# Who computes the second half's input operands, and in which steps

## The chip, the core and the metric

The kernel runs on one core of a Trainium2 chip. A core has a matrix engine (PE), a vector engine (DVE), a scalar engine (ACT), a GpSimd engine (POOL) and a queue engine (SP) that issues DMAs; they run side by side, each in the order of its own queue, and wait for each other by semaphores. The metric is the device time of one execution in microseconds (us), the median of several runs. The engines work on SBUF (128 partitions); PE writes to PSUM, a small memory with banks of 128x512 floats.

## The reference

A gate g mixes two branches over the same input x (2048 tokens, 576 features):

```
g = sigmoid((x * gate_w).sum(-1))
a = linear attention (32 heads, two softmaxes as feature map) @ wo
b = (relu(x @ W_gate) * (x @ W_up)) @ W_down        # 576 -> 4608 -> 576
out = g * a + (1 - g) * b
```

Everything is float32. Branch b is the larger part of the work and the only one that the change touches.

## The kernel before, in words

**Precision.** PE multiplies in a shortened form of float32 ("fp32r"). Each operand is therefore kept as a rounded high part, made by ACT, and a low part (operand minus high part), made by DVE; a product is high x high + high x low + low x high.

**Branch b.** The tokens fall into two halves of 1024, the features into two halves, and the products are done by a scheme of seven block products in place of eight (Strassen's). For this each half of the tokens needs seven operands, made from four blocks of x: the blocks are scaled with a row of square roots of 1 - g (in the tile that the profile calls `ac` here, `sb` in the code), three blocks are used as they are and four operands are differences. Each operand is then split into high and low parts. The operands of the second half are made while the first half is computed, by the generator `second_half` (line 1283 and on): it loads four blocks of 128x512 into `xr` tiles (b11, b12, b21, b22), scales them (line 1311), forms the four differences in place (line 1315), rounds (line 1316, ACT) and forms the low part (line 1296, or 1299 for a third of it), and stores the pair to DRAM (`xod`, 512 KB a time). Both parts pass through one tile `o`, so a new rounding must wait until the store before it has been read out. All of this happens three times, once for each p = 0, 1, 2 (three slices of 128 rows): 12 products with the root row, 12 differences, 21 roundings, 21 low parts, 21 stores.

**Units and steps.** A unit u is one block of 128 hidden features of one half of the tokens; units 0 to 35 are the first half, 36 to 71 the second. A unit has seven steps j = 0 to 6, one for each block product, in function `step`. In a step PE does seven matmuls of the block product (line 1145, into the banks `cx`, `ca`, `cy`) and three to five of the down projection of an earlier unit pair (line 1176, into `pd` and `pm`). DVE, ACT and POOL meanwhile turn finished banks into hidden values and split them (lines 1276, 1281, 1346, 1354, 1404, 1502), add up outputs (1242), and split the weights of coming units (ACT 876 and 1107, DVE 879, 882, 897 to 900, 1110, and POOL 1096 to 1099 for sums of down weights). An even unit has more hidden values to split than an odd one. From unit 36 on the weights are read back from DRAM and this extra work is gone.

**What sets the order.** The whole stage stands in `in_order`: every engine executes its instructions in the order in which the code was traced. An engine doesn't stop at the end of a step; it runs ahead until an instruction's semaphore holds it. At the end of `step` stands the call that advances `second_half`: before the change after steps 3 and 6 of each unit from 4 to 33, 60 calls at most. Between two `yield`s lies what one call issues. One p takes 18 calls, so nine units: the loads (first call), products of t = 0 two calls on, products of t = 1 and the first rounding two calls on, then low part and (difference and) rounding in turn. The last low part comes in unit 30.

Two places where PE can be held matter later: the product of step 6 adds to bank `cx`, which DVE's line 1404 in step 5 has to have read; and the down matmuls of a step need the low part from line 1281 of the step before and a bank that ACT (line 1225) has filled.

Of the kernel before, what the change touches and what calls it, by code (L numbers as in the profile page):

```python
# [1 line left out]

# [7 lines left out]
AF = mybir.ActivationFunctionType  # L10
# [6 lines left out]
TB = 512  # L17
NTB = S // TB
NT = S // P
NC = F // P  # L20
# [63 lines left out]
def gated_mix_kernel(  # L84
# [24 lines left out]
    nc = tc.nc  # L109
    PSUM = bass.MemoryType.PSUM  # L110
    SUB, ADD, MULT = ALU.subtract, ALU.add, ALU.mult
    tt, pt = nc.vector.tensor_tensor, nc.gpsimd.tensor_tensor
# [10 lines left out]
    sbd = dram.tile([P, NTB, TB], F32, name="sbd")  # L123
# [350 lines left out]
    with in_order(tc, nc, nc.gpsimd):  # L474
        for t in range(2, NT - 2):
            if t in (3, 6, 10):
                load_x((t + 2) // 4)
            if t == 8:
                whole(half_gates(0))
                sb = xw.tile([P, 2, TB], F32, name="sb", bufs=1)  # L480
# [180 lines left out]
    t = NT - 1  # L661
# [450 lines left out]
    def rest_weights(g, step):  # L1112

        a = WDR[g, 0][:, 4 * P:].rearrange("p (c q) -> p c q", c=2)
        if step == 0:
            nc.scalar.activation(W4[g][:, 0:2, 0], a, AF.Copy)
        elif step == 1:
            tt(out=W4[g][:, 0:2, 1], in0=a, in1=W4[g][:, 0:2, 0].bitcast(F32), op=SUB)  # L1118
            pt(out=a[:, 0], in0=a[:, 0], in1=a[:, 1], op=ADD)  # L1119
        elif step == 2:  # L1120
            nc.scalar.activation(W4[g][:, 2, 0], a[:, 0], AF.Copy)
            nc.scalar.activation(W4[g][:, 3], W4[g][:, 1].bitcast(F32), AF.Copy, scale=-1.0)
        else:
            tt(out=W4[g][:, 2, 1], in0=a[:, 0], in1=W4[g][:, 2, 0].bitcast(F32), op=SUB)
# [30 lines left out]
    def load_rest(hf):  # L1155
        for t in range(2):
            a = ACC4[hf, t] = sums_of[0][64 * t:64 * (t + 1), 2]
            nc.sync.dma_start(a, att[4 * P:, rows(0, 0, t, hf)[1]])
# [128 lines left out]
    def second_half():  # L1287

        sb = sums_of[2][:, 2]
        ra, rb_ = (xr.tile([P, 3, TB], F32, name="xr", tag="xr") for _ in range(2))  # L1290
        b11, b12, b21, b22 = b = ra[:, 0], ra[:, 1], ra[:, 2], rb_[:, 0]
        o = rb_[:, 1:3].bitcast(F32R)

        def low(n, p, a):
            if p < 2:
                tt(out=o[:, 1], in0=a, in1=o[:, 0].bitcast(F32), op=SUB)
                nc.sync.dma_start(xod[:, n - 1, p::3], o.bitcast(F32))
            else:
                tt(out=o[32:64, 0], in0=a[32:64], in1=o[32:64, 0].bitcast(F32), op=SUB)
                nc.sync.dma_start(xod[:, n - 1, p], o[:, 0].bitcast(F32))  # L1300

        for p in range(3):
            for i, a in enumerate(b):
                k, t = divmod(i, 2)
                nc.sync.dma_start(a, xs[:, k, p, (2 + t) * TB:(3 + t) * TB])
            for t in range(2):
                nc.sync.dma_start(sb, sbd[:, 2 + t])
                yield
                yield
                for a in b[t::2]:  # L1310
                    tt(out=a, in0=a, in1=sb, op=MULT)
            for n, r, a, c in ((1, b11, None, None), (2, b21, None, None), (3, b22, None, None), (5, b11, b12, b11),
                               (7, b12, b22, b12), (6, b22, b22, b11), (4, b21, b21, b22)):
                if a is not None:
                    tt(out=r, in0=a, in1=c, op=SUB)
                nc.scalar.activation(o[:, 0], r, AF.Copy)
                yield
                low(n, p, r)
                yield

    def swap_in(u, j):

# [28 lines left out]
    def gate_last(up, g, made):  # L1351

        if made:
            tt(out=g, in0=up, in1=g, op=MULT)
        else:
            gated(g, up)
        return g
# [31 lines left out]
    def step(u, j):  # L1389


        g, odd = divmod(u, 2)
# [16 lines left out]
        make = 0 < u < NC - 1  # L1409
        old = not odd and g > 0  # L1410

        if j == 0:
            if u > 0:
                a = gate_last(*LATE.pop())
# [85 lines left out]
        elif j == 6:  # L1500
            a = T["g2"]
# [48 lines left out]
        if u == NC + 1:  # L1550
            if j == 6:
                store_rest(0, 0)
                store_rest(0, 1)
                load_rest(1)
        if j in (3, 6) and 4 <= u < NC - 2:
            next(later_half, None)

    later_half = second_half()
    with in_order(tc, nc, nc.tensor, nc.vector, nc.scalar, nc.gpsimd, nc.sync):
        for u in range(len(units)):  # L1560
            for j in range(7):
                step(u, j)
# [152 lines left out]
```

## Time and profile before

| what | value |
|---|---|
| median of 3 runs | 1566.52 us (1566.35 to 1567.34) |
| the profiled execution, its own time | 1565.42 us |
| its span, first to last instruction | 1563.6 us |
| DVE busy | 1247.0 us (80%) |
| ACT busy | 804.9 us (51%) |
| POOL busy | 257.6 us (16%) |
| granted PE clock | 1.000 |

The profiled execution stands 1.1 us below the median, and 1.8 us of it lie outside the span. PE is busy nearly all the time, but its matmuls overlap and their ends are modelled, so lost time is better seen from the times at which matmuls start than from the busy share. DVE's share of 80% is a mean: it is over 90% of the time busy while the weights are split (units 0 to 35, from about 330 to 920 us) and about 70% afterwards.

### The profile page before, as it was taken

The numbers are of one execution on the slowest core, as the hardware profiler recorded it, in microseconds if no ns is written. First come the engines' busy times: TensorE is split into PE (matmuls) and PEld (weight loads), VectorE is DVE, ScalarE is ACT, GpSimd is POOL, SyncE is SP. The second block draws the span as 40 slices with busy tenths as digits, with TensorE's granted clock in tenths as the row PEclk, the third lists the DMA queues.
The fourth block names the chain that finished last, engine by engine and source line by source line (L and its number), as shares of the span: only waits on it lengthen the run. The fifth ranks groups of instructions, "written<-read, shape, count | busy, mean of one in ns | idle before, by whom it ended". The sixth has DMA issues, their size and how long they took to land.

```text
span 1563.6 us, 21083 instructions
## 1 busy us (share of the span) xinstructions
PE 1549.0 (99%) x7715; PEld 1290.6 (83%) x7715; DVE 1247.0 (80%) x1985; ACT 804.9 (51%) x1418; POOL 257.6 (16%) x400
## 2 busy tenths in 40 slices
PE   9999999999999999999999999999999999999998
PEld 9999995687878787888777888888888888888886
DVE  4997776499999999999999878677677677677676
ACT  4344335566777777777777764333333333333332
POOL 0126522111111111111111111111111111111110
PEclk9999999999999999999999999999999999999999
DMA  5364404696755575567545537633433433433432
GB/s 174 107 208 178 167 30 151 187 356 278 251 219 221 217 267 224 205 234 262 206 191 222 201 120 286 240 134 142 189 133 146 187 133 140 192 134 143 191 134 67
DMA packets 67075, 291.84 MB, mean 187 GB/s; under 512 B 7538, under 2 KB 9074, under 8 KB 57372
## 3 DMA queue, kind: packets, MB, share of 16 engines
q1 hardware_dynamic: 63756, 278.73, 48.1%
q0 software_dynamic: 2352, 10.11, 2.0%
q10 hardware_dynamic: 864, 1.65, 0.3%
q8 instruction: 61, 1.00, 0.2%
q14 instruction: 42, 0.34, 0.1%
HBM read 176.78 MB, written 112.27 MB: 185 GB/s over the span
## 4 chain that ended last, share of the span: by engine, by line
PE 78%; DVE 17%; issue 2%; DMA 1%; ACT 1%; POOL 0%; SPq 0%; DVEq 0%; POOLq 0%; ACTq 0%
PE cx L1145 23%; PE pd L1176 17%; PE ca L1145 11%; PE cy L1145 5%; PE kv L176 4%; PE pk L176 3%; PE pq L176 3%; PE pm L1176 3%; DVE hl L1281 2%; DVE ac L1242 2%; DVE ws L879 1%; DVE g L1346 1%; PE kv L423 1%; PE po L564 1%; DVE ws L882 1%
## 5 line engine op out<-in xcount | busy, mean ns | idle before, releaser
L1176 PE MATMUL pd<-hh,wd 128*128 128x512 f32 x980 | 382.0, 390 | 1.6 <-ACT pd L1225 1.6
L1191 DVE TENSOR_TENSOR ac<-pd,ac 128x512 f32<-128x512 f32 x238 | 164.5, 691 | 139.3 <-PE pd L1176 139.3
L1145 PE MATMUL cx<-xo,wb 128*128 128x512 f32 x1008 | 253.6, 391 | 3.9 <-DVE u L1404 3.8
L1276 ACT ACTIVATE hh<-g 128x512 fp32r<-128x512 f32 x249 | 148.3, 623 | 204.7 <-DVE g L1346 187.2
L1145 PE MATMUL cx<-xo,ws 128*128 128x512 f32 x1008 | 252.1, 389 | 0.5 <-ACT cy L1400 0.5
L1145 PE MATMUL ca<-xo,ws 128*128 128x512 f32 x1008 | 252.0, 389 | 0.0
L1145 PEld LDWEIGHTS cx<-xo,wb 128*128 128x128 f32 x1008 | 188.0, 188 | 48.8 <-DVE u L1404 10.4
L1145 PEld LDWEIGHTS cx<-xo,ws 128*128 128x128 f32 x1008 | 189.0, 188 | 40.5 <-ACT cy L1400 1.3
L1145 PEld LDWEIGHTS ca<-xo,ws 128*128 128x128 f32 x1008 | 189.2, 188 | 39.4
L1176 PEld LDWEIGHTS pd<-hh,wd 128*128 128x128 f32 x980 | 183.9, 188 | 42.2 <-ACT pd L1225 4.1
L1176 PE MATMUL pd<-hl,wd 128*128 128x512 f32 x490 | 190.9, 390 | 0.0
L1281 DVE TENSOR_TENSOR hl<-g,hh 128x512 fp32r<-128x512 f32 x249 | 171.3, 688 | 0.2 <-ACT hh L1276 0.2
L1107 ACT ACTIVATE wd<-wdr 128x384 fp32r<-128x384 f32 (+1 forms) x143 | 80.6, 565 | 114.0 <-PE pm L1176 114.0
L1145 PE MATMUL cy<-xo,wb 128*128 128x512 f32 x504 | 125.9, 389 | 0.0
L1096 POOL TENSOR_TENSOR wdr<-wdr 128x128 f32<-128x128 f32 x70 | 32.8, 468 | 510.3 <-DVE wd L1110 510.3
L1145 PEld LDWEIGHTS cy<-xo,wb 128*128 128x128 f32 x504 | 94.6, 188 | 19.6
L1176 PEld LDWEIGHTS pd<-hl,wd 128*128 128x128 f32 x490 | 92.0, 188 | 19.5 <-DVE hl L1281 0.9
L1242 DVE TENSOR_TENSOR ac<-pd,ac 128x512 f32<-128x512 f32 x114 | 78.2, 686 | 28.8 <-PE pd L1176 28.2
L1346 DVE TENSOR_TENSOR g<-g,g 128x512 f32<-128x512 f32 x140 | 96.4, 689 | 2.4
L1361 ACT ACTIVATE g<-cx 128x512 f32<-128x512 f32 x73 | 43.6, 598 | 100.9 <-PE cx L1145 99.9
L1119 POOL TENSOR_TENSOR wdr<-wdr 128x64 f32<-128x64 f32 x35 | 11.5, 328 | 485.1 <-DVE wd L1118 476.4
L1110 DVE TENSOR_TENSOR wd<-wdr,wd 128x384 fp32r<-128x384 f32 (+1 forms) x143 | 88.4, 619 | 2.1 <-ACT wd L1107 1.0
(261 smaller groups left out, 2704.3 us busy)
## 6 DMA issues: line engine op xcount, KB each, us to landing
wsd<-ws SPq DMA_DIRECT2D x34, 1280.0 KB
ws<-wsd SPq DMA_DIRECT2D x34, 1280.0 KB
wbd<-wb SPq DMA_DIRECT2D x34, 960.0 KB
wb<-wbd SPq DMA_DIRECT2D x34, 960.0 KB
wr<-wgu SPq DMA_DIRECT2D x36, 768.0 KB
wdr<-wd SPq DMA_DIRECT2D x36, 320.0 KB
wdr<-wd SPq DMA_DIRECT2D x36, 256.0 KB
xo<-xod SPq DMA_DIRECT2D x7, 1280.0 KB
```

Source lines behind the costliest of these rows:

```text
L176: nc.tensor.matmul(ps, w, m, start=i == 0, stop=i == len(pairs) - 1)
L1096: pt(out=a[:, 2], in0=a[:, 2], in1=a[:, 3], op=ADD)
L1107: nc.scalar.activation(o[:, 0], a, AF.Copy)
L1110: tt(out=o[:, 1], in0=a, in1=o[:, 0].bitcast(F32), op=SUB)
L1145: nc.tensor.matmul(ps, w, v, start=first and m == 0, stop=m == len(pairs) - 1, skip_group_check=True)
L1176: mm = lambda ps, w, v, a, z: nc.tensor.matmul(ps, w, v, start=a, stop=z, skip_group_check=True)
L1191: tt(out=a, in0=ps, in1=a, op=ADD)
L1242: tt(out=a, in0=ps, in1=a, op=ADD)
L1276: nc.scalar.activation(h, src, AF.Copy)
L1281: tt(out=l, in0=src, in1=h.bitcast(F32), op=SUB)
L1346: tt(out=b, in0=a, in1=b, op=SUB)
L1361: nc.scalar.activation(a, ps, AF.Copy)
```

## The change

`second_half` is rewritten. It now lists 30 items, ten for each p, and each item has three parts: make, high, low. The items of one p are: the loads; the products with the first root row; the products with the second; then operands 1, 2, 3, 5, 7, 6, 4. The products and the differences ("make") go to POOL (`pt` in place of `tt`); the roundings ("high") stay on ACT and the low parts on DVE. The items are issued in twos, in four calls for each unit pair: in an even unit the make of the first item after step 4 and its high after step 6; in the following odd unit after step 0 the low of the first item and the make of the second, after step 2 the high and the low of the second. So a p takes five unit pairs in place of nine units, and the last low part comes in unit 33. The five pairs of a p are called A (loads; products with row 1), B (products with row 2; operand 1), C (operands 2 and 3), D (5 and 7) and E (6 and 4) below. The line numbers of the changed kernel are 1 higher up to second_half, and 19 higher behind it.

```diff
-        for p in range(3):
-            for i, a in enumerate(b):
-                k, t = divmod(i, 2)
-                nc.sync.dma_start(a, xs[:, k, p, (2 + t) * TB:(3 + t) * TB])
-            for t in range(2):
-                nc.sync.dma_start(sb, sbd[:, 2 + t])
-                yield
-                yield
-                for a in b[t::2]:
-                    tt(out=a, in0=a, in1=sb, op=MULT)
-            for n, r, a, c in ((1, b11, None, None), (2, b21, None, None), (3, b22, None, None), (5, b11, b12, b11),
-                               (7, b12, b22, b12), (6, b22, b22, b11), (4, b21, b21, b22)):
-                if a is not None:
-                    tt(out=r, in0=a, in1=c, op=SUB)
-                nc.scalar.activation(o[:, 0], r, AF.Copy)
-                yield
-                low(n, p, r)
-                yield
+        def items():
+            nothing = lambda: None
+            for p in range(3):
+                def load():
+                    for i, a in enumerate(b):
+                        k, t = divmod(i, 2)
+                        nc.sync.dma_start(a, xs[:, k, p, (2 + t) * TB:(3 + t) * TB])
+                    nc.sync.dma_start(sb, sbd[:, 2])
+
+                def scaled(t):
+                    for a in b[t::2]:
+                        pt(out=a, in0=a, in1=sb, op=MULT)
+                    if t == 0:
+                        nc.sync.dma_start(sb, sbd[:, 3])
+
+                yield load, nothing, nothing
+                for t in range(2):
+                    yield partial(scaled, t), nothing, nothing
+                for n, r, a, c in ((1, b11, None, None), (2, b21, None, None), (3, b22, None, None),
+                                   (5, b11, b12, b11), (7, b12, b22, b12), (6, b22, b22, b11), (4, b21, b21, b22)):
+                    yield (partial(pt, out=r, in0=a, in1=c, op=SUB) if a is not None else nothing,
+                           partial(nc.scalar.activation, o[:, 0], r, AF.Copy), partial(low, n, p, r))
+
+        every = items()
+        for make, high_, low_ in every:
+            make()
+            yield
+            high_()
+            yield
+            low_()
+            make, high_, low_ = next(every)
+            make()
+            yield
+            high_()
+            low_()
+            yield
...
-        if j in (3, 6) and 4 <= u < NC - 2:
-            next(later_half, None)
+        if 4 <= u < NC - 2 and j in ((0, 2) if odd else (4, 6)):
+            next(later_half)
```

What stands on the engines now is shown at unit 20 and the start of unit 21, a pair D of the second p. `wdr` are the down weights, `wr` the raw weights of the next unit, `xr` the blocks of x. First POOL, before: the four sums of down weights of unit 20 and the first ones of unit 21.

```order
L1096 TENSOR_TENSOR wdr_6531<-wdr_6531 128x128
L1097 TENSOR_TENSOR wdr_6531<-wdr_6531 128x128
L1098 TENSOR_TENSOR wdr_6531<-wdr_6531 128x128
L1099 TENSOR_TENSOR wdr_6531<-wdr_6531 128x128
L1119 TENSOR_TENSOR wdr_6680<-wdr_6680 128x64
L1096 TENSOR_TENSOR wdr_6680<-wdr_6680 128x128
```

POOL at the same place, with the change:

```order
L1097 TENSOR_TENSOR wdr_6522<-wdr_6522 128x128
L1098 TENSOR_TENSOR wdr_6522<-wdr_6522 128x128
L1099 TENSOR_TENSOR wdr_6522<-wdr_6522 128x128
L1100 TENSOR_TENSOR wdr_6522<-wdr_6522 128x128
L1328 TENSOR_TENSOR xr<-xr 128x512
L1334 TENSOR_TENSOR xr<-xr 128x512
L1120 TENSOR_TENSOR wdr_6672<-wdr_6672 128x64
```

The two differences of the pair, issued after step 4 of unit 20 and after step 0 of unit 21, stand directly one behind the other in POOL's queue, right behind the sums of unit 20: nothing of another step lies between them.

Then DVE in unit 20, before, from the sums of weights (step 2) to the read of `cx` in step 5:

```order
L900 TENSOR_TENSOR wr<-wr 128x384
L1346 TENSOR_TENSOR g_6468<-g_6615,g_6468 128x512
L1281 TENSOR_TENSOR hl<-g_6436,hh 128x512
L1315 TENSOR_TENSOR xr<-xr 128x512
L1242 TENSOR_TENSOR ac<-pd_6707,ac 128x512
L1281 TENSOR_TENSOR hl<-g_6615,hh 128x512
L879 TENSOR_TENSOR ws<-wr,ws 128x4x256
L882 TENSOR_TENSOR ws<-wr,ws 32x4x128
L1404 TENSOR_TENSOR u_6733<-cx,u_6733 128x512
```

and with the change:

```order
L901 TENSOR_TENSOR wr<-wr 128x384
L1365 TENSOR_TENSOR g_6460<-g_6609,g_6460 128x512
L1282 TENSOR_TENSOR hl<-g_6430,hh 128x512
L1243 TENSOR_TENSOR ac<-pd_6699,ac 128x512
L1282 TENSOR_TENSOR hl<-g_6609,hh 128x512
L880 TENSOR_TENSOR ws<-wr,ws 128x4x256
L883 TENSOR_TENSOR ws<-wr,ws 32x4x128
L1423 TENSOR_TENSOR u_6725<-cx,u_6725 128x512
```

The difference of line 1315 is gone from DVE's queue; all else keeps its order. Last, DVE from the end of unit 20 into unit 21, before:

```order
L1349 SCALAR_TENSOR_TENSOR g_6745<-g_6745,u_6733 128x512
L1296 TENSOR_TENSOR xr<-xr 128x512
L1354 TENSOR_TENSOR g_6777<-cx,g_6777 128x512
L879 TENSOR_TENSOR wb<-wr,wb 128x3x256
L882 TENSOR_TENSOR wb<-wr,wb 32x3x128
L1110 TENSOR_TENSOR wd<-wdr_6680,wd 128x384
```

and with the change, from step 0 to step 3 of unit 21 (a row of "L1297" is a low part):

```order
L1297 TENSOR_TENSOR xr<-xr 128x512
L880 TENSOR_TENSOR wb<-wr,wb 128x3x256
L883 TENSOR_TENSOR wb<-wr,wb 32x3x128
L1111 TENSOR_TENSOR wd<-wdr_6672,wd 128x384
L1119 TENSOR_TENSOR wd<-wdr_6672,wd 128x2x64
L1243 TENSOR_TENSOR ac<-pd_6859,ac 128x512
L898 TENSOR_TENSOR wr<-wr 128x384
L899 TENSOR_TENSOR wr<-wr 128x384
L900 TENSOR_TENSOR wr<-wr 128x384
L901 TENSOR_TENSOR wr<-wr 128x384
L1297 TENSOR_TENSOR xr<-xr 128x512
L1282 TENSOR_TENSOR hl<-g_6767,hh 128x512
```

The low parts have moved from the ends of units to steps 0 and 2 of the odd unit; line 1315, which stood in step 3 of unit 21 too, is gone there as well.

More of the change, by code (lines that the diff above doesn't have):

```diff
@@ L1 @@
 from contextlib import ExitStack, contextmanager
+from functools import partial
 import concourse.bass as bass
```

## The prediction

> **What bounds the kernel now.** I start with the page and then take the stage that the change touches, units 4 to 33, beside an equally long one of the second half, by stretches.
>
> ```profile
> PE 1549.0 (99%) x7715; PEld 1290.6 (83%) x7715; DVE 1247.0 (80%) x1985; ACT 804.9 (51%) x1418; POOL 257.6 (16%) x400
> 403.00:911.00 508.00, 502.84 (x2193) 409.30 (x2192) 473.13 (x741) 376.18 (x643) 71.75 (x131) 1.00 0.58 219
> 960.00:1468.00 508.00, 508.00 (x2243) 420.65 (x2242) 362.19 (x593) 171.81 (x338) 68.03 (x140) 1.00 0.44 165
> ```
>
> PE (first pair after the length) starts 2193 matmuls in the first stretch and 2243 in the second: 50 fewer in the same 508 us, at the same clock of 1.00. DVE (third pair) is busy 473 us of 508 in the first, 362 in the second; POOL hardly at all. PE is the bound, and it loses some 2% where DVE is almost full. The waits of PE in that stage name who holds it:
>
> ```profile
> PE cx L1145 <- DVE u L1404: 3.5, 9, 1.0
> PE pd L1176 <- ACT pd L1225: 1.6, 5, 0.4
> ```
>
> Both wait for the ends of even units. Each such wait also costs a refill, so I measure the loss from the starts of the first matmul of step 6 in even units (start, us, operation):
>
> ```profile
> 407.97 1.75 PE L1145 MATMUL cx<-xo,wb 128*128 128x512 f32 x7
> 443.00 1.87 PE L1145 MATMUL cx<-xo,wb 128*128 128x512 f32 x7 [1.02 <-DVE u L1404]
> 476.66 1.75 PE L1145 MATMUL cx<-xo,wb 128*128 128x512 f32 x7
> 511.09 1.88 PE L1145 MATMUL cx<-xo,wb 128*128 128x512 f32 x7 [0.16 <-DVE u L1404]
> 614.46 1.88 PE L1145 MATMUL cx<-xo,wb 128*128 128x512 f32 x7
> 648.46 1.88 PE L1145 MATMUL cx<-xo,wb 128*128 128x512 f32 x7 [0.15 <-DVE u L1404]
> 889.00 1.75 PE L1145 MATMUL cx<-xo,wb 128*128 128x512 f32 x7
> 922.55 1.75 PE L1145 MATMUL cx<-xo,wb 128*128 128x512 f32 x7
> ```
>
> The last two rows are units 32 and 34: no second-half work, no wait, 33.55 us for a unit pair. From unit 4 to unit 34 are 15 pairs: 922.55 - 407.97 = 514.58, less 15 x 33.55 = 503.25. **11.3 us** are lost in the stage, and no more can be won there.
>
> How the loss hangs on DVE follows from the same rows. DVE last idles in step 1 of an odd unit (the wait for `pd` below) and is then busy without a gap until line 1404 of the next even unit. What second_half put into that stretch, at 0.60 us an instruction (677.93, 678.53, 679.13 below), against the pair's loss: units 7 and 8, one low part, 0.6 us: lost 33.66 - 33.55 = 0.11. Units 17 and 18, a low part and a difference, 1.2 us: 0.45. Units 9 and 10, two differences and a low part, 1.8 us: 0.88. Units 5 and 6, four products, 2.4 us: 1.48. I use the line **loss = 0.9 x (work - 0.65)**, a little above these points so that the sum comes out: of the fifteen periods two carry nothing, two one instruction, three two, six three and two four, and 0.4 + 3 x 0.5 + 6 x 1.04 + 2 x 1.58 = 11.3, as measured.
>
> **The change part by part.** 24 instructions leave DVE (12 products, 12 differences), and the 21 low parts move to steps 0 and 2 of odd units. The question is what 24 instructions on POOL cost DVE. Rows of an earlier stage, where POOL and DVE scale parts of one tile:
>
> ```profile
> 48.87 1.19 POOL L210 TENSOR_TENSOR e<-e,sm 128x576 f32<-128x576 f32 x1 [9.13 <-DVE sm L277]
> 49.25 1.42 DVE L210 TENSOR_TENSOR e<-e,sm 128x576 f32<-128x576 f32 x1
> 115.20 0.76 DVE L210 TENSOR_TENSOR e<-e,sm 128x576 f32<-128x576 f32 x1
> 115.33 1.67 POOL L210 TENSOR_TENSOR e<-e,sm 128x576 f32<-128x576 f32 x1 [3.39 <-PE ptr L381]
> ```
>
> Whoever starts first takes its own time (POOL 1.19, DVE 0.76), and the other is longer by what was left: DVE starts at 49.25 and ends at 50.67, so its 0.76 began at 49.91, 0.15 before POOL's end at 50.06; at 115.33 POOL's 1.19 began at 115.81, 0.15 before DVE's end. They don't share, they take turns. In unit 20:
>
> ```profile
> 675.00 0.66 POOL L1098 TENSOR_TENSOR wdr<-wdr 128x128 f32<-128x128 f32 x1
> 675.74 0.66 POOL L1099 TENSOR_TENSOR wdr<-wdr 128x128 f32<-128x128 f32 x1
> 674.52 0.82 DVE L897 TENSOR_TENSOR wr<-wr 128x384 f32<-128x384 f32 x1
> 675.37 0.70 DVE L898 TENSOR_TENSOR wr<-wr 128x384 f32<-128x384 f32 x1
> 676.11 0.70 DVE L899 TENSOR_TENSOR wr<-wr 128x384 f32<-128x384 f32 x1
> 676.85 0.56 DVE L900 TENSOR_TENSOR wr<-wr 128x384 f32<-128x384 f32 x1
> 677.33 0.68 DVE L1346 TENSOR_TENSOR g<-g,g 128x512 f32<-128x512 f32 x1
> 677.93 0.68 DVE L1281 TENSOR_TENSOR hl<-g,hh 128x512 fp32r<-128x512 f32 x1
> 678.53 0.68 DVE L1315 TENSOR_TENSOR xr<-xr 128x512 f32<-128x512 f32 x1
> 679.13 0.68 DVE L1242 TENSOR_TENSOR ac<-pd,ac 128x512 f32<-128x512 f32 x1
> ```
>
> Lines 897 to 899 take 0.70 to 0.82 beside POOL's sums, line 900 alone 0.56: the same turns, with short partners.
>
> The Trainium skill, "SBUF — State Buffer", section "Who interferes with whom", has this as a rule: a VectorE instruction with two SBUF inputs and a GpSimd instruction that reads SBUF lock each other out, the second one fully, for the whole instruction. The trace agrees (0.76 becomes 1.42). By the rule the price grows with POOL's instruction and the sum is the one below; by a fixed price, as the short rows alone could be read, it is the rival that ends faster.
>
> No row has a 128x512 product on POOL, but three widths bound it:
>
> ```profile
> L1096 POOL TENSOR_TENSOR wdr<-wdr x70: 458/463/774, 351.5 to 1515.7; 128x128 f32<-128x128 f32 x70
> L343 POOL TENSOR_TENSOR xb<-xb x8: 1834/1846/1856, 155.1 to 179.0; 128x768 f32<-128x768 f32 x8
> ```
>
> From 0.46 for 128 to 1.84 for 768 is 2.16 ns an element, so 512 take **1.28 us**, nearest to the row of the same kind (a difference in place, line 343); the 1.19 for 576 with a broadcast operand would give 1.05, the low end.
>
> Now pair D at unit 20, with the order of the changed program: both differences stand behind line 1099 on POOL and wait for nothing. The first is ready at about 676.45 (the sums follow each other at 0.08), gets its turn 0.14 before line 899 ends (676.67) and ends at 677.95. Line 900 runs from 677.80 to 678.36 in place of 677.41: 0.95 late. The second difference runs from 678.22 to 679.50; line 1346 runs from 679.36 to 680.04 in place of 678.01: **2.03 late**. So a pair of POOL instructions costs DVE 2.0 us, 1.0 each, where a difference on DVE cost 0.60. And both fall before line 1404 of the even unit, also the one that the code issues in the odd unit.
>
> Work in the stretch with the change, by pair:
> - B: no low part in the odd unit before (A's steps issue none), two products: 2.0 us, loss 0.9 x 1.35 = 1.2.
> - C: one low part (operand 1): 0.6 us, loss 0.1.
> - D and E: one low part and two differences: 2.6 us, loss 1.78 each.
> - A: one low part, and two products that wait for their loads. The weights' store is issued at 672.87 in unit 20 (below), the loads behind it; 960 and 1,280 KB at the 382 GB/s of the stretch below take 6 us, so POOL starts near 679.5 to 680. Line 879, at 680.33 in unit 20, stands 1.2 earlier in A, which carries two DVE instructions less in the stretch; so it has the turn (1.22 long), line 882 waits for the first product, line 1404 reads PSUM and passes, as line 1242 passed at 0.68 beside POOL's sums in this unit (673.32). One product counts: 1.6 us, loss 0.86; in the first A without the low part 0.3. Its ends are 0.1 and 2.1.
>
> ```profile
> 672.87 0.33 SPq L1469 DMA_DIRECT2D wbd<-wb  x1
> 680.33 1.22 DVE L879 TENSOR_TENSOR ws<-wr,ws 128x1024 fp32r<-128x1024 f32 x1
> 602.00:608.75 6.75, 6.75 (x31) 5.58 (x31) 6.64 (x11) 5.92 (x12) 2.67 (x4) 1.00 1.02 382
> 673.32 0.68 DVE L1242 TENSOR_TENSOR ac<-pd,ac 128x512 f32<-128x512 f32 x1
> ```
>
> Sum: B 3 x 1.2 = 3.7, C 0.3, D and E 6 x 1.78 = 10.7, A 0.3 + 2 x 0.86 = 2.0, the last period 0.1: 16.8 us in place of 11.3, **5.5 us slower**.
>
> Costed at nothing, with its cover: the low part of step 0 fills DVE's wait for ACT, and what it or ACT's earlier rounding adds goes into the wait for PE in step 1 (unit 17):
>
> ```profile
> 618.75 0.96 DVE L879 TENSOR_TENSOR wb<-wr,wb 128x768 fp32r<-128x768 f32 x1 [0.62 <-ACT wb L876]
> 622.05 0.69 DVE L1242 TENSOR_TENSOR ac<-pd,ac 128x512 f32<-128x512 f32 x1 [0.99 <-PE pd L1176]
> ```
>
> Without that cover it would count 0.6 more in a stretch. The 21 roundings stay on ACT and find it idle (1.53 us at 623.64, below). The DMAs are the same in number; the row loads wait for products that end long before SP needs its next turn. The stretch from unit 30 to 33 costs only E's share, since the operands are read back in unit 35.
>
> **The rivals.**
> 1. *A fixed price* (ends faster). If a POOL instruction holds DVE by 0.26 us, as line 897 to 899 against 900 show, whatever its width, the pairs carry 0.5 (B) and 1.1 (D, E): 6 x 0.9 x 0.47 + 0.4 + 0.4 = 3.3 us of loss, 8.0 faster, 1558.5 us. For it: the nine short POOL instructions of every unit pair hardly show. Against it: the 0.66 us that the long row cost at 49.25. With price x for each instruction the loss is 18.9x - 2.3, so it decides at x = 0.72. At x = 0 nearly all 10 us come back (1556).
> 2. *A shorter product.* With 1.05 us on POOL the price is 0.78 and the loss 12.4: 1 us slower, 1567.6, within what can be told. For it: the row of 1.19. Against it: that row reads a broadcast operand.
> 3. *The store.* The second rounding of a pair waits for the store of the first, two steps earlier. Behind 768 and 256 KB of weights, 512 KB more from 618.5 on at 329 to 382 GB/s end near 623.1 (SP and ACT in unit 17):
>
> ```profile
> 618.02 0.46 SPq L872 DMA_DIRECT2D wr<-wgu  x1
> 618.50:626.25 7.75, 7.75 (x36) 6.42 (x35) 6.33 (x11) 5.65 (x11) 2.32 (x5) 1.00 0.95 329
> 623.64 0.60 ACT L1361 ACTIVATE g<-cx 128x512 f32<-128x512 f32 x1 [1.53 <-PE cx L1145]
> 626.39 0.84 PE L1145 MATMUL cx<-xo,ws 128*128 128x512 f32 x3
> ```
>
> ACT idles until 623.64, and PE needs that copy only at 626.39, so the rounding (0.61) may start 2 us late. If the store landed 3 us later than I think, nine odd units would each lose 1 us: 1581. Against it: the loads are all issued early.
>
> **How the numbers follow.** The forecast is 1565.42 + 5.5 = 1570.9 for the profiled execution, which stood 1.1 under the median: **1572.0**. Its upper bound is 1.28 us, POOL's whole length, for each instruction (loss 21.9, 1577); its lower edge is rival 2. A measurement of this kernel tells 0.2%, 3.1 us, from no change. Chances: forecast 0.60, rival 2 0.17, rival 1 with price zero 0.17, rival 3 0.06. The range from 1561 to 1577 leaves out rival 3 and most of rival 1. Slower by over 0.2%: 0.62; within: 0.21 (rival 2 and the forecast's low edge); faster: 0.17.
>
> **What would show it.** Line 901 and line 1365 of the changed kernel (900 and 1346 of before) at 1.2 to 1.8 us in the even units of B, D and E; pairs of 33.65 us for C and about 35.3 for D and E; PE waiting for line 1282 (low parts of hidden values) and for line 1423; DVE's busy time hardly smaller though 24 x 0.685 = 16.4 us left it. Wrong would be: DVE's rows at their old lengths beside `xr` rows of POOL, POOL rows of a microsecond or less, or ACT idle before line 1336 for a DMA.

## The result, and the profile after

| | before | after |
|---|---|---|
| median of 6 runs | 1566.43 us (1564.75 to 1567.38) | 1572.13 us (1571.01 to 1573.77) |
| ratio, 95% interval | 1 | 1.0038 (1.0026 to 1.0051) |
| the profiled execution: time, span | 1565.42, 1563.6 us | 1572.18, 1570.4 us |
| DVE busy, instructions | 1247.0 us, 1985 | 1254.8 us, 1961 |
| POOL busy, instructions | 257.6 us, 400 | 295.1 us, 424 |

The changed kernel is 5.7 us slower. The page's busy times of the changed kernel:

```profile
PE 1548.8 (99%) x7715; PEld 1290.8 (82%) x7715; DVE 1254.8 (80%) x1961; ACT 805.4 (51%) x1418; POOL 295.1 (19%) x424
```

24 instructions have gone from DVE to POOL, and DVE is busy longer than before. The stage of units 4 to 33 in the table by stretches (length, then PE, PEld, DVE, ACT and POOL):

```profile
403.00:911.00 508.00, 496.95 (x2168) 404.85 (x2167) 474.58 (x706) 373.38 (x637) 109.23 (x155) 1.00 0.59 219
```

In the same 508 us PE started 2168 matmuls in place of 2193, and DVE needs 474.58 us for 706 instructions where it needed 473.13 for 741 (24 of the 35 fewer now run on POOL, the others come later because the kernel is behind). The waits of PE in that stage (us in total, times, longest):

```profile
PE pd L1177 <- DVE hl L1282: 8.6, 9, 1.3
PE cx L1146 <- DVE u L1423: 2.4, 9, 0.3
```

PE no longer waits for ACT there but for DVE's line 1282, nine times, once in each of the nine pairs that carry two POOL instructions in an even unit. The starts of step 6 in even units (start, us, operation; units 4, 6, 8, 16, 18, 20, 22 and 34):

```profile
408.98 0.39 PE L1146 MATMUL cx<-xo,wb 128*128 128x512 f32 x1
443.87 1.90 PE L1146 MATMUL cx<-xo,wb 128*128 128x512 f32 x7 [0.27 <-DVE u L1423]
477.59 1.75 PE L1146 MATMUL cx<-xo,wb 128*128 128x512 f32 x7
616.94 1.88 PE L1146 MATMUL cx<-xo,wb 128*128 128x512 f32 x7 [0.27 <-DVE u L1423]
650.62 1.75 PE L1146 MATMUL cx<-xo,wb 128*128 128x512 f32 x7
685.91 1.88 PE L1146 MATMUL cx<-xo,wb 128*128 128x512 f32 x7 [0.27 <-DVE u L1423]
722.13 1.19 PE L1146 MATMUL cx<-xo,wb 128*128 128x512 f32 x4 [0.25 <-DVE u L1423]
929.34 0.39 PE L1146 MATMUL cx<-xo,wb 128*128 128x512 f32 x1
```

From unit 4 to unit 34: 929.34 - 408.98 = 520.36, less 15 x 33.55 = 503.25: **17.1 us** lost, where it was 11.3. Each difference of neighbours less 33.55 is a pair's loss (unit 6 is a B, 443.87 - 408.98 - 33.55 = 1.34; unit 18 a C, 0.13; unit 20 a D, 1.74; unit 22 an E, 2.67):

| pair | predicted loss | measured |
|---|---|---|
| B, three times | 1.2 | 1.34, 1.34, 1.34 |
| C, three times | 0.1 | 0.17, 0.13, 0.17 |
| D, three times | 1.78 | 1.75, 1.74, 2.01 |
| E, three times | 1.78 | 1.89, 2.67, 2.11 |
| A, second and third | 0.86 | 0.17, 0.15 |
| unit 34 | 0.1 | 0.13 |

The other 1.0 us between the two profiled executions was there before the stage (unit 4 starts at 408.98 and 407.97), and the rest from unit 34 on is the same (1570.4 - 929.34 = 641.06, 1563.6 - 922.55 = 641.05). From the first product of branch b (at 337.07 and 336.01) to that step both take 71.9 us, and the profiled executions of all runs below start the step at 407.1 to 410.0: 1.0 us is a difference between executions.

Unit 20 of the changed kernel, the timeline of DVE, of POOL, and of PE:

```profile
677.52 0.70 DVE L900 TENSOR_TENSOR wr<-wr 128x384 f32<-128x384 f32 x1
678.26 1.53 DVE L901 TENSOR_TENSOR wr<-wr 128x384 f32<-128x384 f32 x1
679.71 1.78 DVE L1365 TENSOR_TENSOR g<-g,g 128x512 f32<-128x512 f32 x1
681.42 0.68 DVE L1282 TENSOR_TENSOR hl<-g,hh 128x512 fp32r<-128x512 f32 x1
677.15 0.66 POOL L1100 TENSOR_TENSOR wdr<-wdr 128x128 f32<-128x128 f32 x1
677.77 1.60 POOL L1328 TENSOR_TENSOR xr<-xr 128x512 f32<-128x512 f32 x1
679.45 1.50 POOL L1334 TENSOR_TENSOR xr<-xr 128x512 f32<-128x512 f32 x1
682.15 0.50 PE L1177 MATMUL pd<-hl,wd 128*128 128x512 f32 x1 [1.00 <-DVE hl L1282]
```

The rows are to be read as a chain. POOL's first difference is issued at 677.77, but DVE's line 900 has the turn until 678.22; 0.14 before that POOL gets going, and ends at 679.37: 1.29 of its own. DVE's line 901, issued at 678.26 and alone 0.56 long, is held until then (1.53). The second difference waits for line 901 and takes 1.30 from 679.65 to 680.95; line 1365, alone 0.68, takes 1.78. Line 1282 comes two microseconds late, and PE has waited 1.00 for it.

### The profile page after: what moved, and what is told of

It reads as the page before. It is cut to its first block, busy times and chain, and to the rows that moved or that the text cites. A ratio compares the mean times of both kernels' runs of the same rounds, so it can differ in the third digit from the quotient of the medians.

```text
span 1570.4 us, 21092 instructions
## 1 busy us (share of the span) xinstructions
PE 1548.8 (99%) x7715; PEld 1290.8 (82%) x7715; DVE 1254.8 (80%) x1961; ACT 805.4 (51%) x1418; POOL 295.1 (19%) x424
## 4 chain that ended last, share of the span: by engine, by line
PE 82%; DVE 13%; issue 1%; DMA 1%; ACT 1%; POOL 0%; SPq 0%; DVEq 0%; ACTq 0%; POOLq 0%
PE cx L1146 25%; PE pd L1177 18%; PE ca L1146 12%; PE cy L1146 6%; PE kv L177 4%; PE pk L177 3%; PE pq L177 3%; PE pm L1177 3%; DVE ac L1243 2%; DVE hl L1282 2%; DVE g L1365 1%; PE kv L424 1%; DVE ws L880 1%; PE pv L239 1%; PE po L565 1%
## 5 line engine op out<-in xcount | busy, mean ns | idle before, releaser
L1365 DVE TENSOR_TENSOR g<-g,g 128x512 f32<-128x512 f32 x140 | 103.0, 736 | 2.4
L1111 DVE TENSOR_TENSOR wd<-wdr,wd 128x384 fp32r<-128x384 f32 (+1 forms) x143 | 91.7, 642 | 1.7 <-ACT wd L1108 0.6
```

What stands on the lines that cost most here:

```text
L1365: tt(out=b, in0=a, in1=b, op=SUB)
```

## The experiments

Each is made from the changed kernel unless it says otherwise; times are medians, with the lowest and the highest run behind them; the intervals are those of the ratio to the kernel before, measured on the same chip beside them (1565.54 us for the first four runs, 1565.87 for the last four).

**Who makes, in which steps.** The change does two things: other engine, other steps. Two runs separate them. In the first, VectorE does the work in the new steps:

```diff
-                        pt(out=a, in0=a, in1=sb, op=MULT)
+                        tt(out=a, in0=a, in1=sb, op=MULT)
...
-                    yield (partial(pt, out=r, in0=a, in1=c, op=SUB) if a is not None else nothing,
+                    yield (partial(tt, out=r, in0=a, in1=c, op=SUB) if a is not None else nothing,
```

> The changed kernel with the 12 products and 12 differences back on DVE, all else as changed (steps, roundings, low parts). Theory (POOL and DVE take turns): a difference or product costs DVE 0.60 us instead of 1.0, and those of odd units (step 0) fall into DVE's idle time of steps 0 and 1. Work in the stretch: A 0.6 us, B 1.2, C 0.6, D and E 1.2 each, so losses of about 0.1, 0.5, 0.1, 0.5, 0.5 us; 5 us in all in place of 17: 1560 us, faster than the kernel before. Rival (the new steps of roundings and low parts do the harm): about 1572 us as the changed kernel.

Measured: 1561.06 us (1558.94 to 1562.49), ratio 0.9965 (0.9952 to 0.9978); unit 4 to 34 from 407.36 to 915.91, 5.3 us lost. In the second, the kernel before keeps its steps and gives products and differences to GpSimd:

```diff
-                    tt(out=a, in0=a, in1=sb, op=MULT)
+                    pt(out=a, in0=a, in1=sb, op=MULT)
...
-                    tt(out=r, in0=a, in1=c, op=SUB)
+                    pt(out=r, in0=a, in1=c, op=SUB)
```

> The kernel before with the 12 products and 12 differences on POOL, in the old steps. Theory: each lies behind POOL's sums of step 3 and costs DVE 1.0 us in place of 0.60, in odd and even units; by loss = 0.9 x (work - 0.65) the fifteen pairs lose 20.5 us in place of 11.3: 1575 to 1576 us. Rival (the steps do it): 1566.5 us as before. Rival (a fixed price of 0.26 us): 1561 us or so.

Measured: 1575.7 us (1574.88 to 1576.67), ratio 1.0061 (1.0044 to 1.0077); 409.16 to 932.94, 20.5 us lost. PE's waits in the stage, first with VectorE in the new steps, then with GpSimd in the old ones:

```profile
PE cx L1146 <- DVE u L1423: 2.3, 6, 0.4
```

```profile
PE pd L1176 <- DVE hl L1281: 7.8, 8, 1.3
PE cx L1145 <- DVE u L1404: 2.1, 6, 0.5
PE pd L1176 <- ACT pd L1225: 0.4, 1, 0.4
```

The wait for the low part of hidden values goes with GpSimd, in the old steps as in the new. By the medians the new steps alone gain 4.5 us and GpSimd alone, in the old steps, costs 10.2, and the change's 5.7 is the sum of both. By the losses in the stage the two are 6.0 and 9.2, and GpSimd costs more in the new steps (17.1 - 5.3 = 11.8) than in the old, so the sum is not exact.

**What a GpSimd instruction costs, by its length.** The same instructions on a quarter of the columns, so that the last 384 columns of each block are left unscaled and undifferenced:

```diff
-                        pt(out=a, in0=a, in1=sb, op=MULT)
+                        pt(out=a[:, :P], in0=a[:, :P], in1=sb[:, :P], op=MULT)
...
-                    yield (partial(pt, out=r, in0=a, in1=c, op=SUB) if a is not None else nothing,
+                    yield (partial(pt, out=r[:, :P], in0=a[:, :P], in1=c[:, :P], op=SUB) if a is not None else nothing,
```

> The changed kernel with products and differences on the first 128 of 512 columns only (the other columns of the operands are left as loaded). Theory: the price follows POOL's length, 0.46 us in place of 1.28, so two instructions hold DVE for 0.4 us in place of 2.0: pairs D and E carry 1.0 us and lose 0.3, the others 0.1 or so; 1558 us. Rival (a fixed price for each POOL instruction, whatever its length): 1572 us. Rival (steps): 1572 us.

Measured: 1556.88 us (1555.26 to 1557.98), ratio 0.994 (0.9925 to 0.9955), 1.9 us lost in the stage. And with products and differences left out altogether, loads, roundings, low parts and stores kept:

```diff
-                    for a in b[t::2]:
-                        pt(out=a, in0=a, in1=sb, op=MULT)
...
-                    yield (partial(pt, out=r, in0=a, in1=c, op=SUB) if a is not None else nothing,
+                    yield (nothing,
```

> The changed kernel without products and differences (the operands are the blocks as loaded); loads, roundings, low parts and stores in the new steps. Theory: each stretch carries one low part, pairs lose 0.1 us: 1557 us, the floor of this arrangement. Rival (steps): 1570 us or more. Rival (the store): ACT's second rounding of a pair still waits for the store of the first, and pairs C, D and E lose up to 1 us each: 1560 to 1565 us.

Measured: 1555.2 us (1554.59 to 1557.14), ratio 0.9932 (0.9917 to 0.9947), 0.3 us lost. The same place in the run with a quarter of the columns (DVE, then POOL):

```profile
670.06 0.70 DVE L901 TENSOR_TENSOR wr<-wr 128x384 f32<-128x384 f32 x1
670.69 0.95 DVE L1365 TENSOR_TENSOR g<-g,g 128x512 f32<-128x512 f32 x1
669.58 0.78 POOL L1328 TENSOR_TENSOR xr<-xr 128x128 f32<-128x128 f32 x1
670.43 0.65 POOL L1334 TENSOR_TENSOR xr<-xr 128x128 f32<-128x128 f32 x1
```

With 128 columns DVE's two rows are 0.14 and 0.27 above their own 0.56 and 0.68; with 512 columns they were 0.97 and 1.10 above. The number of instructions is the same, so a price for each instruction, whatever its width, is ruled out: DVE pays for POOL's length.

**Reading or merely being there.** Each product and each difference is replaced by two clearings of the same 128x512 block on GpSimd, which write SBUF and read nothing; the operands are then zero:

```diff
-                        pt(out=a, in0=a, in1=sb, op=MULT)
+                        for _ in range(2):
+                            nc.gpsimd.memset(a, 0.0)
...
-                    yield (partial(pt, out=r, in0=a, in1=c, op=SUB) if a is not None else nothing,
+                    yield (partial(clear, r) if a is not None else nothing,
```

(`clear` does the same two clearings on r.)

> The changed kernel with each product and each difference replaced by two clearings of the same 128x512 block on GpSimd, which write SBUF and read nothing (the operands are zero). Theory (VectorE and GpSimd take turns only where GpSimd reads SBUF): lines 901 and 1365 keep their lengths of 0.5 to 0.8 us beside the clearings, stage loss under 3 us, 1555 to 1558. Rival (any GpSimd instruction on SBUF holds VectorE for its length): two clearings of about 0.5 us each cost VectorE about as much as one difference, lines 901 and 1365 reach 1.2 us or more, 1565 to 1572.

Measured: 1554.81 us (1554.34 to 1556.78), ratio 0.9931 (0.9917 to 0.9944), 0.75 us lost in the stage. Unit 20, DVE and POOL (line 1371 is line 1365 of the changed kernel):

```profile
671.15 0.56 DVE L901 TENSOR_TENSOR wr<-wr 128x384 f32<-128x384 f32 x1
671.63 0.69 DVE L1371 TENSOR_TENSOR g<-g,g 128x512 f32<-128x512 f32 x1
672.23 0.69 DVE L1282 TENSOR_TENSOR hl<-g,hh 128x512 fp32r<-128x512 f32 x1
670.65 2.16 POOL L1308 MEMSET xr<- 128x512 f32 x4
```

POOL wrote SBUF from 670.65 to 672.81 right beside three DVE instructions with two inputs from SBUF, and none of them is longer than alone. The time is 0.2 us under the expected range. So it is a GpSimd instruction that reads SBUF which a DVE instruction with two SBUF inputs can't run beside; one with a single SBUF input passes (line 1423, 0.69 us beside GpSimd's products in unit 14, shown further down). The Trainium skill, "SBUF — State Buffer", section "Who interferes with whom", states the same: a VectorE instruction with two SBUF inputs contends with a GpSimd instruction that reads SBUF, not with one that only writes it. The traces agree with both halves: 1.53 and 1.78 us beside the differences of the changed kernel, 0.56 and 0.69 beside the clearings of this run.

**The step in the code, or the moment.** Two runs move the first make of a pair from step 4 of the even unit to step 6, behind line 1423, and leave the loads where they are:

```diff
-            make()
+            if getattr(make, "__name__", "") == "load":
+                make()
             yield
+            if getattr(make, "__name__", "") != "load":
+                make()
             high_()
```

In the first run the products and differences stay on GpSimd.

> The changed kernel with the first item's make on GpSimd moved in the code from step 4 to step 6 of the even unit. GpSimd's queue holds no other instruction between the two places, so it runs ahead to the same moment. Theory (what costs is when GpSimd reads SBUF, and this is set by its queue and its semaphores, not by the step in which the code issues it): no change, stage loss about 17, 1571 to 1573 us. Rival (the step in the code decides, the engine starts the difference after line 1423): losses of D and E fall to about 1, 1560 to 1564.

Measured: 1571.84 us (1571.31 to 1572.55), ratio 1.0039 (1.0023 to 1.0054), 16.3 us lost. The timeline of unit 20 (POOL, DVE; line 1368 is line 1365 of the changed kernel):

```profile
677.53 1.61 POOL L1332 TENSOR_TENSOR xr<-xr 128x512 f32<-128x512 f32 x1
679.22 1.49 POOL L1337 TENSOR_TENSOR xr<-xr 128x512 f32<-128x512 f32 x1
678.03 1.53 DVE L901 TENSOR_TENSOR wr<-wr 128x384 f32<-128x384 f32 x1
679.49 1.78 DVE L1368 TENSOR_TENSOR g<-g,g 128x512 f32<-128x512 f32 x1
```

The same collision at the same lines: GpSimd had nothing else in its queue and ran ahead to it. In the second run VectorE does the work in these steps (the edit above, and `tt` for `pt`); on VectorE, whose queue is full, the place in the code is the place in time.

> The changed kernel with products and differences on VectorE, and the first item's make moved from step 4 to step 6 of the even unit, behind line 1423. Theory (only second-half work between step 1 of an odd unit and line 1423 of the next even unit costs, by 0.9 x (work - 0.65)): one low part of 0.6 us is left there in each pair, about 0.1 us a pair, 1.5 to 2 us in the stage against 5.3 with VectorE in the steps of the change: 1557 us, 1556 to 1559. Rival (the gap of 0.62 + 0.99 us around the end of the even unit is already full, so that two differences and a low part there come out late in step 1 instead): the loss stays at about 5 us, 1560 to 1561.

Measured: **1556.69 us** (1554.84 to 1558.03), ratio 0.994 (0.9927 to 0.9952), 0.46 us lost from unit 4 (409.96) to unit 34 (913.67): the fastest of the versions that compute everything, 15 us under the changed kernel and 9 under the kernel before. DVE from the end of unit 20 into unit 21:

```profile
680.42 0.68 DVE L1332 TENSOR_TENSOR xr<-xr 128x512 f32<-128x512 f32 x1
681.02 0.68 DVE L1376 TENSOR_TENSOR g<-cx,g 128x512 f32<-128x512 f32 x1
681.80 0.69 DVE L1297 TENSOR_TENSOR xr<-xr 128x512 fp32r<-128x512 f32 x1
682.41 0.69 DVE L1337 TENSOR_TENSOR xr<-xr 128x512 f32<-128x512 f32 x1
683.34 0.96 DVE L880 TENSOR_TENSOR wb<-wr,wb 128x768 fp32r<-128x768 f32 x1 [0.25 <-ACT wb L877]
...
685.82 0.69 DVE L1243 TENSOR_TENSOR ac<-pd,ac 128x512 f32<-128x512 f32 x1 [0.16 <-PE pd L1177]
```

Two differences and a low part stand where DVE used to wait 0.62 us for ACT and 0.99 for PE; 0.25 and 0.16 of the waits are left, and PE waits for no DVE line in the whole stage. DVE is busy 1247.7 us, as much as in the kernel before: the work didn't shrink, it moved to where nobody waits.

**The store.** In the changed kernel the second rounding of a pair (line 1336) waits for the first operand's store. Here operands 2, 5 and 6 are rounded but not stored, and their partners 3, 7 and 4 are stored to both places, so that three operands hold the wrong block and the DMAs are as many:

```diff
+            places = {2: (), 5: (), 6: (), 3: (2, 3), 7: (5, 7), 4: (6, 4)}.get(n, (n,))
...
-                nc.sync.dma_start(xod[:, n - 1, p::3], o.bitcast(F32))
+                for m in places:
+                    nc.sync.dma_start(xod[:, m - 1, p::3], o.bitcast(F32))
```

> The changed kernel in which the first operand of pairs C, D and E (2, 5, 6) is rounded but not stored, and the second (3, 7, 4) is stored to both places, so that those three operands hold the wrong block and no rounding waits for a store issued two steps before. Theory (in E, and in unit 22 above all, the excess over 1.8 us comes from the second rounding's wait for the store): E falls from 1.9, 2.7 and 2.1 to about 1.8 each, stage loss 17.1 to about 16, 1571 us. Rival (the excess comes from the turns on SBUF or from the weights' loads): E stays at 1.9 to 2.7 and the time at 1572.

Measured: 1570.63 us (1570.05 to 1571.6), ratio 1.003 (1.0019 to 1.0041); 407.59 to 927.06, 16.2 us lost. ACT's waits for the store are gone, and unit 22 loses 1.89 in place of 2.67. The third slice's pairs stay at 2.0 (D) and 2.1 (E), though 1.8 was expected of E. The run with the late make on GpSimd keeps the stores and yet lost only 1.94 in unit 22. There the rounding came sooner (ACT and DVE in unit 21; line 1339 is line 1336 of the changed kernel):

```profile
695.83 0.63 ACT L1339 ACTIVATE xr<-xr 128x512 fp32r<-128x512 f32 x1 [2.49 <-DMA xod<-xr]
696.50 0.69 DVE L1297 TENSOR_TENSOR xr<-xr 128x512 fp32r<-128x512 f32 x1
```

The store had been issued at 689.39, so the rounding followed it by 6.4 us, against 7.2 in the changed kernel (below), and DVE didn't wait for it. How late this store is thus differs from run to run. It cost unit 22 about 0.8 us in the profiled execution of the changed kernel, and nothing that shows elsewhere.

## Why the prediction was right

**The price.** It rested on turns: whoever comes second waits until the other's instruction is done. Unit 20 came out as worked out there: POOL's own time 1.29 and 1.30 (estimated 1.28), line 901 1.53 and line 1365 1.78 long (1.2 to 1.8 were named), DVE two microseconds late. In the B pairs the collision came one line earlier than named: in unit 16 it is lines 900 and 901 that take 1.54 and 1.53. That DVE's busy time would hardly fall turned out stronger: it rose by 7.8 us. Without products and differences, and with the same 1961 instructions on DVE, DVE is busy 1232.2 us. So the 24 instructions that left took 14.8 us with them, and 22.6 us of waiting came in, which the records count as busy. (The 16.4 us of the prediction adds up records of 0.685 us that overlap; from one instruction to the next it is 0.60.)

**The line from DVE's work to PE's loss.** It held for D (1.78 for 1.75, 1.74, 2.01) and for C, and was a little low for B (1.2 for 1.34). It also gave the totals of the first two runs: 5 expected for 5.3 with VectorE in the new steps, 20.5 for 20.5 with GpSimd in the old ones. For a low part alone it is too high: about 1.5 us were expected of the run without products and differences and 1.5 to 2 of the late make on VectorE, and 0.3 and 0.46 were measured.

**Pair A was mis-sized**: 0.86 predicted, 0.16 measured. The prediction put POOL's start for the products at 679.5 to 680 of unit 20, early enough to hold line 882 (now 883). The second A, unit 14, shows what happened (DVE, then POOL):

```profile
580.23 0.68 DVE L883 TENSOR_TENSOR ws<-wr,ws 32x512 fp32r<-32x512 f32 x1
580.95 0.69 DVE L1423 TENSOR_TENSOR u<-cx,u 128x512 f32<-128x512 f32 x1
581.55 1.07 DVE L1282 TENSOR_TENSOR hl<-g,hh 128x512 fp32r<-128x512 f32 x1
582.54 1.77 DVE L1111 TENSOR_TENSOR wd<-wdr,wd 128x512 fp32r<-128x512 f32 x1
580.42 3.34 POOL L1314 TENSOR_TENSOR xr<-xr,ac 128x512 f32<-128x512 f32 x2 [4.75 <-DMA ac<-sbd]
```

The products waited for the root row's load until 580.42, after line 883 had its turn. Line 1423 reads a PSUM bank and one tile of SBUF and passes at 0.69; lines 1282 and 1111 behind it pay 0.39 and 1.09, where PE doesn't wait. POOL's products came 0.19 us after the start of line 883, and that decided: only the low part counts. The first A's 0.3 was added to the stage although it lies ahead of unit 4's step 6, where nothing changed.

**Pair E was a little small**: 1.78 for 1.89, 2.67 and 2.11. For unit 22 the third rival named the cause, the store, though it doubted it. The changed kernel's timeline of SP, ACT and DVE in unit 21:

```profile
685.19 0.33 SPq L1496 DMA_DIRECT2D wsd<-ws  x1
689.61 0.38 SPq L1298 DMA_DIRECT2D xod<-xr  x1
696.79 0.63 ACT L1336 ACTIVATE xr<-xr 128x512 fp32r<-128x512 f32 x1 [3.24 <-DVE wr L901]
697.46 0.69 DVE L1297 TENSOR_TENSOR xr<-xr 128x512 fp32r<-128x512 f32 x1 [0.71 <-ACT xr L1336]
```

The store `xod` was issued at 689.61, and ACT stood idle for 3.24 us, to 696.79, 7.2 after that. The profile names line 901, but the rounding reads no weights, and among the waits for ACT line 1336 has this one:

```profile
ACT xr L1336 <- DMA xod<-xr: 10.9, 7, 2.3
```

DVE waited 0.71 us for this rounding, about what unit 22 lost more than the first E (2.67 for 1.89). With the store out of the way, or 0.8 us quicker, DVE's wait and the excess are both gone, so it was the store. "ACT idle before line 1336 for a DMA" was one of the prediction's own signs of being wrong; it came, and it cost these 0.8 us. The prediction let the store land 4.6 us after the weights began to load, counting 768 and 256 KB of weights ahead of it; the store of 1280 KB that is issued ahead of those (`wsd`) it didn't count. Whether that alone makes the landing late wasn't tried. The two microseconds of slack that it found took up most of the delay.

The third slice's D and E lose 0.2 to 0.3 more than the first's, also in the run with partner stores (2.0 and 2.1), so the store isn't why. The trace shows a difference on DVE: the low part of that slice is line 1300, on 32 partitions. Here is the low part ahead of the first D and of the third, each with the instruction behind it:

```profile
488.22 0.68 DVE L1297 TENSOR_TENSOR xr<-xr 128x512 fp32r<-128x512 f32 x1
488.82 0.69 DVE L1282 TENSOR_TENSOR hl<-g,hh 128x512 fp32r<-128x512 f32 x1
835.22 0.68 DVE L1300 TENSOR_TENSOR xr<-xr 32x512 fp32r<-32x512 f32 x1
835.93 0.69 DVE L1282 TENSOR_TENSOR hl<-g,hh 128x512 fp32r<-128x512 f32 x1
```

Line 901 ahead of them starts at 487.74 and 834.63. So from line 901 to line 1282 DVE needs 1.08 us with line 1297 and 1.30 with line 1300, though it works on a quarter of the partitions. These 0.22 us lie in the stretch that counts, and by the prediction's line they are 0.2 us of loss; it had priced all low parts at 0.60. The third B, which has no low part in its stretch, loses 1.34 like the other two. No run changes line 1300 alone.

**The sum**: 16.8 predicted, 17.1 measured. A was 1.4 too large for two pairs and 0.3 for the first; E, B and the third D were too small by 1.3, 0.4 and 0.2. The mechanism was right, but that errors of 1.7 us in one direction and 1.9 in the other nearly cancel is luck. The edits costed at nothing cost nothing: without products and differences, but with the low parts and the roundings in their new steps, 0.3 us is lost in the whole stage.

**The rivals.** A fixed price is refuted by the quarter width. The shorter product is refuted by POOL's own 1.29 for a difference, and by the B pairs, which hold products alone and lost 1.34, more than forecast. The store is real, but worth under 1 us.

## What to carry to other kernels

An engine that is only 16% busy isn't free: before work is moved to it, look in the trace for what its instructions do to the ones that run beside them, and price them by that (1.0 us of DVE for each here, where DVE itself needed 0.60). Where an engine is the limit only in stretches, first move work within it, to its own waits: that took 9 us off this kernel. Giving the work to GpSimd instead of VectorE in the steps of the change cost 11. Moving its code later didn't delay GpSimd here, whose queue was empty: it ran as soon as its inputs were there (1571.84 us for 1572.13).

## What the runs showed that was not expected

The prediction priced a GpSimd instruction by its length alone. The clearings show that it also matters what it does: four of 128x512, which only write SBUF, ran 2.16 us beside DVE rows at 0.56, 0.69 and 0.69 and held none of them. DVE's records count the wait for its turn as busy, so that DVE's share is the same (80%) in the kernel before, the changed one and the fastest one, at 1566, 1572 and 1557 us. And a low part on 32 partitions took more of DVE's time than one on 128, by 0.22 us.
